# q and k loaded token group first and turned on TensorE, one activation table, issue order from a table: an attention and SoLU feed-forward kernel

## The chip, the cores and the metric

The kernel runs on one core of one Trainium2 chip. The metric is the device time of one execution in microseconds, taken as the median of several runs. The profile is one further execution, recorded by the hardware profiler.

A core has five engines with a queue of instructions each: TensorE (PE; its weight loads are shown apart as PEld), VectorE (DVE), ScalarE (ACT), GpSimd (POOL) and SyncE (SP, which here only issues DMAs). Sixteen DMA engines move data between the chip's memory (HBM) and the on-chip buffer (SBUF). Matmul results land in PSUM, which DVE and ACT read. Each engine works through its queue in order, and an instruction whose semaphore has not come holds up what is queued behind it.

## The reference

Two stages follow each other. The first is attention with 4 batches, 8 heads, 768 tokens and a head size of 64. A query sees the first 8 keys (global) and the 96 keys up to itself (local), with a bias that falls with distance by a slope for each head. The second takes the 3072 x 512 result through a feed-forward layer of width 1024, whose activation is h times softmax(h), followed by a layer norm without offset and a second matrix.

```python
scores = scale * np.matmul(q, k.transpose(0, 1, 3, 2))
...
scores = scores + bias[None, :, :, :]
scores = np.where(keep, scores, -1000000000.0)
...
a = a / (np.sum(a, axis=-1, keepdims=True) + 1e-09)
return np.matmul(a, v).astype(np.float32)
...
h = x @ w_in
h_max = np.max(h, axis=-1, keepdims=True)
e = np.exp(h - h_max)
sm = e / (np.sum(e, axis=-1, keepdims=True) + 1e-09)
solu = h * sm
mu = np.mean(solu, axis=-1, keepdims=True)
var = np.mean((solu - mu) ** 2, axis=-1, keepdims=True)
ln = (solu - mu) / np.sqrt(var + 1e-06) * g_ln
return (ln @ w_out).astype(np.float32)
```

## The kernel before, in words

The work is cut into 12 units: 4 batches of 3 stretches of 256 tokens. Unit `21` is batch 2, stretch 1. All arithmetic on TensorE is in fp16 with fp32 sums. Every piece of work is a step with a name, and steps of unit `21` carry `.21`.

**Loads.** `lq` and `lk` (L296 to L302) each issue two DMAs on SP, one for the even and one for the odd head of each pair. A DMA moves 128 pieces of 2 KB: a piece is 8 tokens (R) of one head, and there are 4 head pairs and 32 token groups. On the source side the pairs are outermost, `j g (r d)`, so partition p holds pair p // 32 and group p % 32. `lv` (L304) issues two DMAs of 1024 pieces of 256 bytes. Each load has two buffers.

**Turning q and k.** `cq` and `ck` (L313) cast to fp16, on POOL but for the first unit, which uses DVE. `tq` and `tk` (L362) then issue a crossbar transpose DMA each on ACT's queue: eight 128 x 128 blocks, one for each token of a group, so that head size comes to the partitions. `kn` (L348) puts the tokens of k back in order, with a copy on POOL. q is left in the turned order, and the score matmuls read it with a stride (L421). Scores therefore hold queries in the order (r, g), the masks are built in that order (`pat`, L201), and the output stores (L601) undo it, eight rows of groups outermost. The first unit is turned on TensorE instead (`pq`, `pk`, L333), with `tq` on ACT and `kn` on DVE copying out of PSUM.

**Attention.** `cv` casts v on POOL into `vd`. `ko` and `vo` (L382, L393, DVE) are copies of k and v in which the first columns are replaced by the global keys and values, that `kg` and `vg` keep for each batch. `sc0` to `sc3` (L408) make the scores of a head pair in PSUM, `ex` (ACT) the exponentials, `mu` (DVE) multiplies with the exponential of bias and mask, `av0` and `av1` (L458) multiply with v, a column of ones giving the sums, `xn` (DVE) divides, `xt` (L495) turns the result on TensorE and `xc` (DVE) copies it to `xT`.

**Feed-forward.** `f10` and `f11` (L514) make h, `e2` (ACT, L526) its exponential, `u` (DVE, L531) the product, `s` (L540) the sums of e, u and u squared on TensorE, `st` and `st2` (DVE) the statistics, `rs` (ACT, L577) one over the root by a Ln and an Exp. `f20` and `f21` (L584) apply the second matrix, whose gain and mean have been folded in beforehand (`gw`, `gm`, `gmc`, `gc`), `o0` and `o1` (ACT) scale and copy out of PSUM, `out0` and `out1` (SP) store.

**Weights.** `l_win` and `l_wout` are loads of 2 MB each on SP; `win0` to `win3` and `gw0` to `gw7` bring them to fp16.

**Buffers in PSUM.** A ring of three two-bank tiles serves scores, `av` and h. Two one-bank tiles (`mm`) serve `xt`, `s`, both `f2`, the first unit's `pq` and `pk`, and `gm`.

**Order.** A planner (L50) runs over all steps when the program is built. Each step has an engine, a duration written by hand, what it depends on, which buffers it takes and gives back, and a priority by unit. The planner gives every engine the step that can start first, by priority within a small window, and the steps are issued in that order.

Of the kernel before, what the change touches and what calls it, by code (L numbers as in the profile page):

```python
# [15 lines left out]
P = 128  # L16


class Step:


    def __init__(self, name, eng, dur, emit, deps=(), take=(), give=(), prio=0.0, dma=0.0):
        self.name, self.eng, self.dur, self.emit = name, eng, dur, emit
        self.deps = [d for d in deps if d is not None]
        self.take, self.give = list(take), list(give)
        self.prio, self.dma = prio, dma
        self.start = self.end = None


class Plan:  # L30
# [6 lines left out]
    LAT = 0.08  # L37
    DMA_LAT = 2.0

# [5 lines left out]
    def add(self, *a, **kw):  # L45
        s = Step(*a, **kw)
        self.steps.append(s)
        return s

    def order(self, window=0.12):  # L50
        free = {p: [0.0] * n for p, n in self.pools.items()}
        givers = {}
        for s in self.steps:
            for g in s.give:
                givers[g] = givers.get(g, 0) + 1
        rel = {}
        clock = {}
        dma_free = {}
        left = list(self.steps)
        done = []  # L60
        while left:
            best = {}
            for s in left:
                if any(d.end is None for d in s.deps):
                    continue
                t = clock.get(s.eng, 0.0)
                for d in s.deps:
                    t = max(t, d.end + (self.LAT if d.eng != s.eng else 0.0))
                ok = True
                need = {}  # L70
                for pool, _ in s.take:
                    need[pool] = need.get(pool, 0) + 1
                for pool, n in need.items():
                    f = sorted(x for x in free[pool] if x is not None)
                    if len(f) < n:
                        ok = False
                        break
                    t = max(t, f[n - 1] + self.LAT)
                if ok:
                    best.setdefault(s.eng, []).append((t, s))  # L80
            assert best, "the plan is stuck: " + ", ".join(s.name for s in left[:12])
            pick = None
            for eng, c in best.items():
                t0 = min(t for t, _ in c)
                t, s = min(((t, s) for t, s in c if t <= t0 + window), key=lambda x: (x[1].prio, x[0]))
                if pick is None or t < pick[0]:
                    pick = (t, s)
            t, s = pick
            for pool, key in s.take:
                f = free[pool]  # L90
                i = min((j for j in range(len(f)) if f[j] is not None), key=lambda j: f[j])
                f[i] = None
                self.slot[(pool, key)] = i
            s.start = t
            clock[s.eng] = t + s.dur
            s.end = t + s.dur
            if s.dma:
                b = max(s.end, dma_free.get(s.eng, 0.0)) + s.dma
                dma_free[s.eng] = b
                s.end = b + self.DMA_LAT  # L100
            for g in s.give:
                givers[g] -= 1
                rel[g] = max(rel.get(g, 0.0), s.end)
                if givers[g] == 0:
                    free[g[0]][self.slot[g]] = rel[g]
            left.remove(s)
            done.append(s)
# [5 lines left out]
def kernel(  # L113
# [21 lines left out]
    R = 8  # L135
# [508 lines left out]
```

## Time and profile before

| | |
|---|---|
| median of 3 runs | 307.53 us (307.14 to 310.0) |
| the profiled execution | 309.56 us |
| its span, first to last instruction | 307.8 us |
| mean granted TensorE clock | 0.818 |
| busy: PE, DVE, ACT, POOL | 170.7, 131.0, 129.6, 64.0 us |
| moved by DMA | 35.42 MB in 60421 packets, 49648 of them under 512 B |
| queue of SP's DMAs (q1) | 29.37 MB, 40.6% of 16 engines |
| queue of ACT's crossbar transposes (q10) | 5.77 MB, 33.3% of 16 engines |

A busy time is the sum over an engine's instructions; the span is longer than any of them. The page cuts the span in 40 slices of 7.7 us and gives the busy share of each in tenths. The clock row is what the throttle granted TensorE, 9 for full speed and 5 for half. In a row of a group stand the line, the engine, the operation, what is written and read, the shape, the count, the busy time, the mean duration in ns, the idle time before it and what ended it. In a row of waits stand who waited for what, the total, the number of waits and the longest. SPq and ACTq are the issue queues of SP and ACT.

### The profile page before, as it was taken

The numbers are of one execution on the slowest core, as the hardware profiler recorded it, in microseconds if no ns is written. First come the engines' busy times: TensorE is split into PE (matmuls) and PEld (weight loads), VectorE is DVE, ScalarE is ACT, GpSimd is POOL, SyncE is SP. The second block draws the span as 40 slices with busy tenths as digits, with TensorE's granted clock in tenths as the row PEclk, the third lists the DMA queues.
The fourth block names the chain that finished last, engine by engine and source line by source line (L and its number), as shares of the span: only waits on it lengthen the run. The fifth ranks groups of instructions, "written<-read, shape, count | busy, mean of one in ns | idle before, by whom it ended". The sixth has DMA issues, their size and how long they took to land.

```text
span 307.8 us, 4520 instructions
## 1 busy us (share of the span) xinstructions
PE 170.7 (55%) x1784; PEld 117.0 (38%) x1784; DVE 131.0 (43%) x323; ACT 129.6 (42%) x165; POOL 64.0 (21%) x91
## 2 busy tenths in 40 slices
PE   0143067374703344691704933069888888989871
PEld 0132046151501233450503522046464657567550
DVE  0072068133405232641207232074786877484530
ACT  5130047171700531442006160046858487876562
POOL 7011140223224213423024110442050400000000
PEclk9999997769585957576655869558997999999998
DMA  2449994999999999996999993198540432102022
GB/s 81 115 135 235 133 316 119 133 121 153 117 122 109 131 144 119 165 141 154 121 121 121 171 139 135 76 149 101 130 102 2 103 36 70 36 34 71 0 70 68
DMA packets 60421, 35.42 MB, mean 115 GB/s; under 512 B 49648, under 2 KB 49648, under 8 KB 60400
## 3 DMA queue, kind: packets, MB, share of 16 engines
q1 hardware_dynamic: 37168, 29.37, 40.6%
q10 hardware_dynamic: 23232, 5.77, 33.3%
q8 instruction: 14, 0.23, 0.4%
q14 instruction: 7, 0.06, 0.1%
HBM read 23.07 MB, written 6.29 MB: 95 GB/s over the span
## 4 chain that ended last, share of the span: by engine, by line
DMA 37%; SPq 23%; PE 18%; DVE 8%; issue 5%; POOL 4%; ACT 4%; ACTq 0%; POOLq 0%; DVEq 0%
DMA ldk<-in_k_dram 20%; DMA ldq<-in_q_dram 13%; SPq L300 11%; SPq L307 8%; PE mm L587 7%; PE ring L519 5%; DMA kt<-c16k 4%; PE mm L551 4%; ACT e L437 3%; SPq L246 2%; DVE u L535 2%; POOL c16q L317 1%; DVE xn L491 1%; DVE ko L388 1%; POOL kn L351 1%
## 5 line engine op out<-in xcount | busy, mean ns | idle before, releaser
L519 PE MATMUL ring<-xT,w_in_sb 128*128 128x256 f16 x384 | 52.8, 299 | 17.5 <-DVE xT L506 15.0
L587 PE MATMUL mm<-gw,u 128*128 128x512 f16 x192 | 51.5, 426 | 13.4 <-DVE st L564 12.4
L528 ACT ACTIVATE e<-ring 128x1024 f16<-128x1024 f32 x24 | 24.5, 1023 | 80.0 <-POOL vd L323 18.6
L519 PEld LDWEIGHTS <-w_in_sb 128*128 128x128 f16 x384 | 40.3, 107 | 27.9 <-ACT w_in_sb L257 14.1
L437 ACT ACTIVATE e<-ring 128x1024 f16<-128x1024 f32 (+1 forms) x48 | 42.7, 958 | 15.7 <-PE ring L422 9.5
L535 DVE TENSOR_TENSOR u<-ring,e 128x1024 f16<-128x1024 f32 x24 | 29.1, 1215 | 41.6 <-ACT e L528 41.6
L587 PEld LDWEIGHTS <-u 128*128 128x128 f16 x192 | 20.1, 107 | 39.6 <-issue 24.3
L422 PE MATMUL ring<-qt,kn 64*128 64x128 f16 x192 | 18.1, 248 | 29.3 <-ACT e L437 23.9
L422 PE MATMUL ring<-qt,ko 64*128 64x128 f16 x160 | 16.2, 244 | 23.5 <-DVE u L535 14.4
L447 DVE TENSOR_TENSOR e<-e,mk 128x1024 f16<-128x1024 f16 x32 | 21.4, 683 | 18.2 <-ACT e L437 18.1
L579 ACT ACT_TABLE_LOAD x12 | 15.4, 1283 | 30.5 <-issue 25.7
L317 POOL CAST c16k<-ldk 128x1024 f16<-128x1024 f32 x11 | 11.4, 1040 | 80.7 <-DMA ldk<-in_k_dram 80.7
L351 POOL COPY kn<-kt 128x1024 f16<-128x1024 f16 x11 | 21.4, 1949 | 22.4 <-PE ring L422 20.0
L469 PE MATMUL ring<-vo,e 128*128 128x65 f16 x160 | 14.8, 210 | 19.2 <-DVE e L447 14.3
L551 PE MATMUL mm<-u 128*128 128x129 f16 x192 | 21.8, 238 | 2.5 <-DVE u L535 2.5
L422 PEld LDWEIGHTS <-kn 64*128 64x128 f16 x192 | 11.0, 107 | 30.9 <-issue 25.0
L323 POOL CAST vd<-ldv 128x512 f16<-128x512 f32 x24 | 14.6, 624 | 34.2 <-DMA ldv<-in_v_dram 32.0
L548 PE MATMUL mm<-ones,e 128*128 128x1 f16 x192 | 21.0, 182 | 0.8 <-ACT e L528 0.8
L551 PEld LDWEIGHTS <-u 128*128 128x128 f16 x192 | 19.7, 116 | 2.9 <-DVE u L535 2.9
L422 PEld LDWEIGHTS <-ko 64*128 64x128 f16 x160 | 9.2, 104 | 29.8 <-issue 25.9
L317 POOL CAST c16q<-ldq 128x1024 f16<-128x1024 f32 x11 | 11.8, 1070 | 41.3 <-DMA ldq<-in_q_dram 32.7
L595 ACT ACTIVATE o<-mm,st 128x512 f32<-128x512 f32 x24 | 15.4, 684 | 9.0 <-issue 7.9
(67 smaller groups left out, 219.3 us busy)
## 6 DMA issues: line engine op xcount, KB each, us to landing
ldq<-in_q_dram SPq DMA_DIRECT2D x24, 256.0 KB
ldk<-in_k_dram SPq DMA_DIRECT2D x24, 256.0 KB
ldv<-in_v_dram SPq DMA_DIRECT2D x24, 256.0 KB
out_dram<-o SPq DMA_DIRECT2D x24, 256.0 KB
w_tmp<-in_moe_w_in_dram SPq DMA_DIRECT2D x1, 2048.0 KB
w_tmp<-in_moe_w_out_dram SPq DMA_DIRECT2D x1, 2048.0 KB
qt<-c16q ACTq DMA_TRANSPOSE x11
kt<-c16k ACTq DMA_TRANSPOSE x11
```

Of the source, the lines that this page charges most:

```text
L300: nc.sync.dma_start(out=t[:, m, :], in_=a)
L307: nc.sync.dma_start(out=t[:, a], in_=v[b][:, tok0 + a * P : tok0 + (a + 1) * P, :].rearrange("h t d -> t h d"))
L317: eng.tensor_copy(out=dst.rearrange("p r m d -> p m r d"), in_=src.rearrange("p m (r d) -> p m r d", r=R))
L351: nc.gpsimd.tensor_copy(out=dst, in_=src)
L422: nc.tensor.matmul(out=t[:, 512 * m + P * c : 512 * m + P * (c + 1)], lhsT=lhs, rhs=rhs, start=(c == (1 if po is None else 0)), stop=(c == ...
L437: nc.scalar.activation(out=e[:, :, lo:], in_=t[:, :, lo:], func=AF.Exp, scale=inv_sqrt_d)
L447: nc.vector.tensor_tensor(out=ev, in0=ev, in1=mb, op=ALU.mult)
L519: nc.tensor.matmul(out=t[:, jj, :], lhsT=w_in_sb[:, c, ts(4 * hf + jj, P)], rhs=x[:, c, :], start=(c == 0 and jj % 2 == 0), stop=(c == NCC ...
L528: nc.scalar.activation(out=e2[plan.slot[("e2", f"{U}{hf}")]].rearrange("p j f -> p (j f)"), in_=t, func=AF.Exp)
L535: nc.vector.tensor_tensor(out=o[:, :, 0:P], in0=t, in1=e, op=ALU.mult)
L551: nc.tensor.matmul(out=t[:, a, 0 : P + 1], lhsT=uv[:, jj, a, 0:P], rhs=uv[:, jj, a, 0 : P + 1], start=False, stop=(a == 1 and hf == 1 and ...
L587: nc.tensor.matmul(out=t, lhsT=uu[plan.slot[("u", f"{U}{i // 4}")]][:, i % 4, a, 0:P], rhs=gw[:, i, :], start=(i == 0), stop=(i == NFC - 1))
```

## The change

- `lq` and `lk` put the token groups outermost on the source side, `g j (r d)`, so partition p holds group p // 4 and pair p % 4.
- All units are turned on TensorE: `pq` and `pk` take a `mm` tile each for eight transposes. `tq` (ACT) and `kn` (ACT, in the first unit DVE) copy out of PSUM into token order, reading with a stride. The crossbar transposes, `kt` and POOL's `kn` are gone, `kn` has two buffers instead of three.
- q is in token order now: the score matmuls read 128 neighbouring columns, the masks use plain token order, and an output store is a plain block of 128 rows.
- A step `tab` at the start asks for the table set that has both exponential and logarithm.
- `cvo` on POOL casts v into `vo` directly; `vo` on DVE only puts the global rows in. The two copies of the global columns, one for each half, become one copy with a repeated source.
- `l_win` is issued by ACT, after mask3.
- `f2` no longer waits for `s`; `s` holds the `u` buffers instead.
- The planner is gone. The steps are issued in the order of a written table, `ORDER`, of 603 names, and a buffer goes to the step that asks next, the one longest free first.

The diff, cut to its core:

```diff
+ORDER = """
+tab ident lq.00 dist lk.00 lv.00 ones mask6 mask3 cq.00 mask4 pq.00 mask0 mask2 lq.01 ck.00 mask5 tq.00 pk.00
+lk.01 mask7 kn.00 l_win lv.01 kg.00 ko.00 sc0.00 mask1 cvo.00 sc1.00 ex0.00 sc2.00 ex1.00 sc3.00 mu0.00 l_g
+ex2.00 mu1.00 lk.02 ex3.00 mu2.00 lq.02 cv.00 l_wout mu3.00 vg.00 vo.00 ck.01 av0.00 av1.00 xn0.00 cq.01 pk.01
+xn1.00 kn.01 pq.01 lk.10 win3 win0 xt.00 ko.01 lq.10 xc.00 tq.01 win2 lv.02 win1 sc0.01 cv.01 sc1.01 sc2.01
+ex1.01 cvo.01 ex2.01 f10.00 mu1.01 ex0.01 mu2.01 lv.12 mu0.01 sc3.01 e20.00 f11.00 vo.01 cq.02 ex3.01 u0.00
+ck.02 pq.02 e21.00 lq.11 mu3.01 pk.02 tq.02 u1.00 av0.01 kn.02 lk.21 av1.01 xn0.01 s.00 xn1.01 gw1 gw7 st.00
+xt.01 gw5 ck.10 xc.01 gw3 st2.00 f11.01 gw4 lk.11 ko.02 cq.10 gw6 gw2 f10.01 lq.12 gw0 rs.00 cvo.02 e21.01 gm
+cv.02 e20.01 u1.01 lv.10 pq.10 gmc cv.12 u0.01 sc0.02 tq.10 sc1.02 pk.10 gc0 ex1.02 s.01 kn.10 mu1.02 sc2.02
+sc3.02 ex0.02 kg.10 ko.10 gc4 ex3.02 sc0.10 ex2.02 sc1.10 mu0.02 f20.00 ex1.10 mu3.02 ex0.10 mu2.02 vo.02 sc2.10
...
+f11.32 st.31 st2.31 rs.31 f10.32 e21.32 u1.32 f21.31 e20.32 u0.32 f20.31 o1.31 out1.31 s.32 o0.31 out0.31 f21.32
+st.32 st2.32 rs.32 f20.32 o1.32 out1.32 o0.32 out0.32
+"""
...
+    def run(self, order):
...
+        free = {p: list(range(n)) for p, n in self.pools.items()}
+        issued = set()
+        for name in names:
+            s = by_name[name]
+            assert all(d.name in issued for d in s.deps + s.after), name
             for pool, key in s.take:
...
+                self.slot[(pool, key)] = free[pool].pop(0)
+            s.emit()
+            issued.add(name)
...
-    pat = [[1, R], [R, G]]
+    pat, npat = [[1, P]], [[-1, P]]
...
     def e_tab():
-        pass
...
+        nc.scalar.preload_act_table_set("natural_log_exp_and_others")
+    plan.add("tab", "ACT", e_tab)
...
+    l_win = plan.add("l_win", "ACT", lambda: e_wload(w_tmp, moe_w_in, NCC), after=[c_mask[3]])
...
-            s4 = src[b].rearrange("(j m) s d -> m j s d", m=2)[m]
-            a = s4[:, tok0 : tok0 + QU, :].rearrange("j (g r) d -> j g (r d)", r=R)
-            nc.sync.dma_start(out=t[:, m, :], in_=a)
...
+            s4 = src[b].rearrange("(j m) s d -> m j s d", m=2)
+            for m in range(2):
+                a = s4[m][:, tok0 : tok0 + QU, :].rearrange("j (g r) d -> g j (r d)", r=R)
+                nc.sync.dma_start(out=t[:, m, :], in_=a)
...
+        def e_castvo(U=U, nb=nb):
+            for a in range(nb):
+                nc.gpsimd.tensor_copy(out=vo[plan.slot[("vo", U)]][:, a, :, 0:D], in_=ldv[plan.slot[("ldv", U)]][:, a])
...
-            nc.scalar.dma_start_transpose(out=dst, in_=src.rearrange("p r m d -> p (r m d)"))
...
+        def e_tev(which, eng, U=U):
             t = mm[plan.slot[("m", which + "p" + U)]].bitcast(FP16)
...
+            src = t.rearrange("p (r g j) -> p j g r", r=R, j=NPAIR)
+            d = (qt if which == "q" else kn)[plan.slot[("qt" if which == "q" else "kn", U)]]
+            dst = d.rearrange("p j (g r) -> p j g r", r=R)
+            if eng == "ACT":
+                nc.scalar.copy(out=dst, in_=src)
...
-                        rhs = qv[lo : lo + D, :, j * 32 + 16 * (c // 2) : j * 32 + 16 * (c // 2) + 16]
+                        rhs = qv[lo : lo + D, j, P * (c // 2) : P * (c // 2 + 1)]
...
-                nc.sync.dma_start(out=out[row : row + P, :].rearrange("(g r) c -> r g c", r=R), in_=osb[plan.slot[("o", f"{U}{a}")]])
...
+                nc.sync.dma_start(out=out[row : row + P, :], in_=osb[plan.slot[("o", f"{U}{a}")]])
```

## The prediction

> **What bounds the kernel now.** I read the page's slices first, then the chain and the waits, then busy time by stage. A first digit of the DMA row near 9 says that the copy engines are busy, not that they are all at work, so the stage windows come last.
>
> ```profile
> PE   0143067374703344691704933069888888989871
> ...
> PEclk9999997769585957576655869558997999999998
> DMA  2449994999999999996999993198540432102022
> ...
> DMA 37%; SPq 23%; PE 18%; DVE 8%; issue 5%; POOL 4%; ACT 4%; ACTq 0%; POOLq 0%; DVEq 0%
> ```
>
> Up to slice 26 (200 us) PE comes and goes and DMA is at 9; after it PE is at 8 to 9 and DMA fades. The chain belongs to DMA and to SP's issue queue. Who waits, over the whole run:
>
> ```profile
> POOL c16k L317 <- DMA ldk<-in_k_dram: 80.7, 11, 17.4
> ...
> POOL c16q L317 <- DMA ldq<-in_q_dram: 32.7, 7, 9.2
> POOL vd L323 <- DMA ldv<-in_v_dram: 32.0, 10, 9.5
> ```
>
> The casts wait for the q and k loads. Why those take 9 to 14 us each shows in the windows (PE, PEld, DVE, ACT, POOL busy, then clock, share of the 16 DMA engines, GB/s):
>
> ```profile
> 3.00:6.00 3.00, 0.00 (x0) 0.00 (x0) 0.00 (x0) 1.62 (x4) 2.73 (x22) 1.00 0.24 89
> ...
> 42.00:45.00 3.00, 2.87 (x26) 2.16 (x24) 2.37 (x3) 1.34 (x2) 2.46 (x2) 1.00 1.06 387
> ...
> 304.00:305.50 1.50, 0.00 (x0) 0.00 (x0) 0.00 (x0) 0.00 (x0) 0.00 (x0) 0.92 0.51 186
> ...
> 42.00:212.00 170.00, 84.87 (x791) 55.91 (x790) 62.26 (x158) 55.89 (x70) 44.96 (x42) 0.69 1.01 136
> 212.00:302.00 90.00, 76.35 (x916) 54.55 (x912) 58.41 (x140) 63.10 (x80) 9.58 (x10) 0.98 0.26 60
> ...
> 215.40:284.90 69.50, 59.33 (x750) 42.58 (x749) 49.91 (x118) 49.45 (x61) 7.42 (x7) 0.98 0.27 65
> ```
>
> 3 to 6 us holds only the first q load, whose source has the 4 head pairs outermost: a quarter of the engines, 89 GB/s. 304 to 305.5 holds only output stores, outermost count 8: half. 42 to 45 is w_out, 128 outermost on both sides, 2 KB packets like q's: all 16, 387 GB/s. So the outermost count sets how many engines a copy gets, and one quarter of them carries every q and k byte. From 212 us PE sets the pace: between the xT copies at 215.4 and 284.9 us lie five units (a unit is 256 tokens of a batch), 13.9 us each, with 11.9 us of PE in each.
>
> **The change, part by part.**
>
> *Loads.* With 32 token groups outermost, q and k get 16 engines by the same reading. One load (two DMAs, 0.52 MB) moves in 1.4 us at 387 GB/s instead of 5.4 to 5.9. By the trace's packet records (2 KB median 84 ns, 256 B median 18 ns) a unit needs (512 x 84 + 2048 x 18 + 256 x 84) ns / 16 = 6.3 us of all engines. SP's issues for a unit: four q and k DMAs of 0.55, two v of 1.85 (the first at 3.73 us), two stores of 0.60: 7.1 us. Both fit under a unit of 13 us; without that cover 7.1 us would be the floor of a unit, far from deciding. Stores stand on SP between the loads of later units; four o buffers let one be two units late before an output copy waits.
>
> *Weights.* l_win leaves SP for ACT, behind mask7. Its issue took 2.09 us on SP; queued behind it are mask1 and the first exps, on which mu and av of unit 00 wait. Scores are ready at about 10.5, so the exps lose some 2 us; if the engines are backed up it is up to the 11.6 us of the longest v issue. Unit 00's attention ends at 17.5 while f1 waits for w_in until 22, so 2 us are hidden and 11.6 would cost 7. l_wout moves up on SP, from 33.98 to behind lq.02, about 18.5 (the first six loads' issues to 13.5, l_g 2.5, two loads 2.4): landed near 28, before ACT reaches gw.
>
> *Crossbar transposes out.* 22 issues leave ACT's queue (median 1.25 and 1.41 us, 35 us or less in all), and 22 transfers leave the engines (queue q10, 33.3% of them). POOL loses kn.
>
> *TensorE transposes in.* 22 groups of 8 (the first unit had its own). Warm price: the chain has the eight L501 transposes in 0.45 us, cold the L337 eight in 1.03. A unit pays 0.9 us, on PE, which is the bound: 10 us in all. Each needs one of two mm banks, shared with xt, s and both f2. A bank is held from the first matmul to the end of the copy: 2 x (0.45 + 1.01) + (0.45 + 0.68) + (1.33 + 0.9) + 2 x (1.73 + 0.69), with some 0.15 of crossing each, is 12 us a unit for two banks, so half used. A pq that waits holds every score behind it on PE's queue, and ACT's exps wait for those. Bounds: 0, or one output copy (0.69 us) ahead of each of 22, 15 us. I take 0 as its own term and let the idle share below carry it.
>
> *Evacuations on ACT, strided.* 22 copies. No row has ACT reading PSUM with a stride. Nearest:
>
> ```profile
> L579 ACT ACT_TABLE_LOAD x12 | 15.4, 1283 | 30.5 <-issue 25.7
> ...
> L506 DVE COPY xT<-mm 128x1024 f16<-128x1024 f16 x12 | 8.2, 682 | 3.3 <-PE mm L501 3.3
> ...
> L346 DVE COPY kn<-mm 128x1024 f16<-128x1024 f16 x1 | 1.2, 1225 | 1.1 <-PE mm L337 1.1
> ...
> L342 ACT COPY qt<-mm 128x1024 f16<-128x1024 f16 x1 | 1.0, 1012 | 3.8 <-PE mm L337 3.8
> ```
>
> On DVE the stride costs 1225 against 682, a factor 1.8; on ACT that would be 1.82 us. But DVE's 1225 is its pace for fp32 too (L535, 1215), the 682 a faster form that ACT does not show: its 1024 elements take 1012 in fp16 and 1029 in fp32. So I take 1.01: 22.2 us, and keep 1.82 (17.8 more, 1.6 a unit) and, downward, nothing.
>
> *One table.* 24 loads of 1.283 go (the first stays): 30.8 us of ACT. ACT's sum is 129.6 - 30.8 + 22.2 = 121.0, 10.1 a unit. The load row stands for its whole price: at 209.31 the load, at 210.61 the Ln, 0.02 us later. The Trainium skill, "ScalarE: Activation LUTs", section "What ACT_TABLE_LOAD costs", adds a drain of about 1.38 us to each; by it 63.9 us would come back, an estimate that the starts in this trace do not bear out.
>
> *POOL and DVE.* POOL: 64.0 - 21.4 (kn, 11 x 1.949) + 20 x 0.624 (cvo) = 55. DVE: 131.0 - 7.6 (L395) - 2.9 - 2.3 (eight copies each of L388 and L397, merged) = 118, 9.9 a unit. Both lie beside PE's 12.8. DVE copies do suffer from POOL: L388 takes 0.16 us at the median and 1.94 at worst, beside a kn of 1.9; a cast is 0.62 to 1.04, so the worst shrinks. The masks' multiplies do not: all 32 lie within 669 to 695 ns. Against moving copies to POOL speaks "SBUF — State Buffer" of the Trainium skill, in its single rule on the shared port pair: a DVE instruction with two SBUF inputs should wait for a POOL instruction that reads. With POOL busy a third of the time and half a cast of waiting, that is an estimate of 0.7 us of DVE a unit; by the row it is 0.
>
> *The sum, in span.*
> 1. To the first f1 matmul. Before: 39.66, after the w_in casts at 37.72. After: the q cast at about 6 (9.74 less 4.0 of transfer), k landed at 7.2 (issued by 3.7, 1.4 of transfer, 2 of landing), scores 3.1 us later as before (15.46 to 18.57), xt 7.3 later (25.9 before): 17.5. w_in goes out behind tq.00 and mask7, about 10.5; with the six loads of units 00 and 01 it makes 4.2 MB at 387 GB/s and 1.05 MB of v at 228 (16 x 256 B / 18 ns), 15.5 us from 2.3: 17.8, plus 2 us as the first load has from last packet to cast, plus 2.1 of casts: 22.
> 2. To the first output copy ACT is in front: ten exps 8.9, four e2 4.1, four evacuations 4.0, eight gw 5.2, rs and gmc 1.0: 23, with small waits 24: 46.
> 3. PE: 12 x (11.9 + 0.9) + gm 1.8 = 155; by then done: units 00 and 01 without f2, parts of 02 and 10, gm: 25. Left 130. PE was busy 59.33 of 69.5 there, 0.85; of its waits in 212 to 302 the largest is L422 on ACT's exps, 5.2 us, beside 19.3 us of table loads on ACT. I let half of the idle time go with them: 0.93, 140 us.
> 4. From the last f2: copy 0.69, store and end some 4.3 (5.8 before, from the copy's end at 302.0 to 307.8; one store on 16 engines instead of two on 8 at 186 GB/s saves some 1.5): 5.
>
> 46 + 140 + 5 = 191, less the chance that PE fills earlier in step 2: I take 190. The profiled run took 309.56 for a span of 307.8; the median of the runs, 307.53, is within 0.3 of the span, so 190 stands for both. With no PE idle at all it is 46 + 130 + 5 = 181, and 6 less if the ramp is PE's too: 175. With the old idle share: 46 + 153 + 5 = 204.
>
> **Rivals.**
> - *ACT and the order become the bound.* Strided copies at 1.82 make ACT 11.7 a unit; with mm banks late (up to 15 us) PE stays at 0.85 or below. 204 to 220. For it: in-order queues that each are 75 to 80% full. Against it: none is above PE.
> - *The loads stay narrow*, if the destination counts otherwise than the stores and loads above suggest. Quarter engines then carry 10.9 (q, k) + 2.3 (v) + 1.3 (out) = 14.5 a unit, x 12, plus 10 of weights and some 28 of start and last unit: 212. Against it: the 42 to 45 row.
> - *PE at half clock, ending slower.* 42 to 212 ran at 0.69, with PE idle again and again. If after the change idle gaps keep the clock at 0.5, step 3 is 260 and the whole 311. It decides from 307.5 - 51 = 256 for 130 of work, a mean of 0.51. Against it: 212 to 302 held 0.98 with PE waits of 1.4 us at most.
>
> **How the numbers follow.** Forecast (PE-bound, 175 to 204): 0.74. ACT and order (204 to 220, a tail above): 0.16. Narrow loads: 0.05. Half clock: 0.03; the last 0.02 lies between. The range runs from 175 to 212: it takes in the idle-share bounds and half of the second case, and leaves out about 0.17. Changes under 1% could not be told from none. Faster by over 1% holds all but half clock and a remnant: 0.96; same 0.01; slower 0.03.
>
> **What would show it.** Loads: windows with q or k alone at a DMA share near 1 and over 300 GB/s, casts that no longer wait. Transposes: 176 more on PE at 0.45 for eight. Evacuation: tq and kn at 1.01, not 1.8. Table: one ACT_TABLE_LOAD. Start: first f1 near 22, first output copy near 46. Step 3: PE busy above 0.9 and clock near 1 from 46 on. I am wrong if PE idles over 15% there, if the clock falls below 0.9, or if casts still wait for ldk.

## The result, and the profile after

On one chip the kernel before took 308.76 us (median of 4) and the changed one 180.64 us (median of 4, 179.17 to 182.84): a ratio of 0.583, 95% interval 0.576 to 0.590. One of the four (182.84 us) ran in a slower state of the chip, as did one or two executions of some variants below: the ratios leave such executions out, the medians hold them, and without them no variant's median would move by more than 0.8 us. The forecast was 190.0 with a range of 175 to 212. The profiled execution took 179.17 us with a span of 177.4; all times of day below are in that span.

The slices of the changed kernel, and the shares of its chain:

```profile
PE   0443769799794989999999999999999999999990
...
PEclk9999988999999999999999999999999999999999
DMA  5999999999379779998199400530101111003023
...
PE 63%; ACT 10%; DVE 10%; DMA 9%; issue 3%; SPq 2%; ACTq 0%
```

A slice is now 4.4 us. PE stands at 9 from slice 15 (67 us) to the last but one, where the kernel before stayed at 8 to 9 only after 200 us. The chain, which belonged to DMA and to SP's issue queue, is PE's. DMA is at 9 in slices 1 to 9, comes and goes after that, and is at 5 or less from slice 22 on.

The waits of the whole run (engine, line and what ended the wait: us in total, times, longest):

```profile
ACT e L511 <- PE ring L502: 20.1, 17, 4.1
POOL cq L308 <- PE mm L332: 15.2, 3, 5.2
...
POOL ck L308 <- DMA ldk<-in_k_dram: 6.5, 2, 5.0
```

The k casts, which waited 80.7 us for their loads, now wait 6.5 (the casts of v, whose loads the change left as they were, still wait 19.1). The longest wait is ACT's for PE: the engine that sets the pace is the one waited for. The second says the same of POOL, which may write the next q tile only when PE has turned an earlier one.

The windows (start and end, length, then PE, PEld, DVE, ACT and POOL busy, PE clock, share of the DMA engines, GB/s):

```profile
3.00:6.00 3.00, 0.60 (x6) 0.61 (x7) 0.72 (x1) 0.49 (x2) 2.67 (x20) 1.00 0.99 317
22.00:46.00 24.00, 19.99 (x278) 15.90 (x278) 18.29 (x35) 21.25 (x29) 8.78 (x12) 0.93 0.97 288
46.00:172.00 126.00, 121.63 (x1589) 90.90 (x1589) 96.59 (x240) 85.77 (x119) 38.20 (x47) 1.00 0.42 127
```

From 3 to 6 us the engines carry loads at a share of 0.99 instead of 0.24, and 317 GB/s instead of 89. From 46 to 172 us PE is busy for 121.63 of 126 us, 0.965, at full clock; no other engine is above 0.77.

The rows that price the added and removed work (busy, mean ns | idle before, and what ended it):

```profile
L429 DVE TENSOR_TENSOR e<-e,mk 128x1024 f16<-128x1024 f16 x32 | 24.4, 789 | 4.1 <-ACT e L419 4.1
...
L340 ACT COPY qt<-mm 128x1024 f16<-128x1024 f16 x12 | 12.1, 1012 | 0.7 <-PE mm L332 0.7
...
L332 PE MATMUL mm<-ident,ck 128*128 128x128 f16 x96 | 8.2, 234 | 1.6 <-DVE ck L308 1.3 <-DVE xT L488 0.3
...
L231 ACT ACT_TABLE_LOAD x1 | 1.3, 1283 | 0.7 <-PEq L606 0.7
```

The strided evacuations cost 1.01 us, not 1.82 (kn's eleven: 1016 ns). There is one table load. The 192 transposes of q and k, 96 of each, take 16.4 us of busy time, overlapped matmuls counted in full.

The start, in the chain (start, length, what):

```profile
9.75 10.81 DMA w_tmp<-in_moe_w_in_dram
...
24.53 3.31 PE ring L502 x16
```

w_in goes out at 9.75 and has landed at 20.56; between the two lines shown the chain has ACT evacuate a q tile (from 21.54), cast a part of w_in and take an exponential, and the first f1 matmul comes at 24.53. The last f2 ends at 173.26 and the span at 177.4.

### The profile page after: what moved, and what is told of

The parts are those of the page before. It is cut to its first block, busy times and chain, and to the rows that moved or that the text cites. A ratio compares the mean times of both kernels' runs of the same rounds, so it can differ in the third digit from the quotient of the medians.

```text
span 177.4 us, 4800 instructions
## 1 busy us (share of the span) xinstructions
PE 151.7 (86%) x1960; PEld 113.9 (64%) x1960; DVE 126.6 (71%) x295; ACT 119.2 (67%) x163; POOL 59.6 (34%) x100
## 4 chain that ended last, share of the span: by engine, by line
PE 63%; ACT 10%; DVE 10%; DMA 9%; issue 3%; SPq 2%; ACTq 0%
PE ring L502 24%; PE mm L570 19%; PE mm L534 6%; DMA w_tmp<-in_moe_w_in_dram 6%; ACT e L419 4%; PE ring L404 3%; PE mm L332 3%; DMA ldq<-in_q_dram 3%; PE ring L453 2%; DVE u L518 2%; PE ring L451 2%; DVE e L429 2%; ACT e L511 2%; PE mm L483 2%; SPq L293 1%
## 5 line engine op out<-in xcount | busy, mean ns | idle before, releaser
L502 PE MATMUL ring<-xT,w_in_sb 128*128 128x256 f16 x384 | 46.6, 278 | 4.6 <-DVE xT L488 2.9
L502 PEld LDWEIGHTS <-w_in_sb 128*128 128x128 f16 x384 | 37.6, 99 | 11.1 <-issue 4.7
L570 PE MATMUL mm<-gw,u 128*128 128x512 f16 x192 | 44.7, 379 | 0.0
L570 PEld LDWEIGHTS <-u 128*128 128x128 f16 x192 | 17.9, 98 | 18.5
L429 DVE TENSOR_TENSOR e<-e,mk 128x1024 f16<-128x1024 f16 x32 | 24.4, 789 | 4.1 <-ACT e L419 4.1
L578 ACT ACTIVATE o<-mm,st 128x512 f32<-128x512 f32 x24 | 16.5, 688 | 10.5 <-PE mm L570 10.3
L321 POOL CAST vo<-ldv 128x512 f16<-128x512 f32 x20 | 14.1, 719 | 20.1 <-PE ring L453 15.0
L308 POOL CAST cq<-ldq 128x1024 f16<-128x1024 f32 x11 | 12.3, 1119 | 17.0 <-PE mm L332 15.2
L473 DVE TENSOR_TENSOR xn<-ring,rl 128x512 f16<-128x512 f32 x24 | 16.6, 691 | 0.8
L453 PE MATMUL ring<-vd,e 128*128 128x65 f16 x192 | 14.4, 197 | 2.7 <-DVE e L431 2.4
L534 PEld LDWEIGHTS <-u 128*128 128x128 f16 x192 | 15.9, 96 | 0.8 <-issue 0.4
L531 PEld LDWEIGHTS <-e 128*128 128x128 f16 x192 | 15.9, 96 | 0.6
L308 POOL CAST ck<-ldk 128x1024 f16<-128x1024 f32 x11 | 11.9, 1090 | 11.9 <-DMA ldk<-in_k_dram 6.5
L453 PEld LDWEIGHTS <-e 128*128 128x128 f16 x192 | 12.2, 99 | 5.0 <-DVE e L431 3.4
L340 ACT COPY kn<-mm 128x1024 f16<-128x1024 f16 x11 | 11.2, 1016 | 5.4 <-PE mm L332 5.4
## 6 DMA issues: line engine op xcount, KB each, us to landing
w_tmp<-in_moe_w_in_dram ACTq DMA_DIRECT2D x1, 2048.0 KB, 10.8
```

The costliest lines, as they stand in the source:

```text
L308: eng.tensor_copy(out=dst.rearrange("p r m d -> p m r d"), in_=src.rearrange("p m (r d) -> p m r d", r=R))
L429: nc.vector.tensor_tensor(out=ev, in0=ev, in1=mb, op=ALU.mult)
L453: nc.tensor.matmul(out=o, lhsT=e[:, m, QU * a + P : QU * a + QU], rhs=vd[plan.slot[("vd", U)]][:, a, h, :], start=(first_in_bank and not t ...
L502: nc.tensor.matmul(out=t[:, jj, :], lhsT=w_in_sb[:, c, ts(4 * hf + jj, P)], rhs=x[:, c, :], start=(c == 0 and jj % 2 == 0), stop=(c == NCC ...
L531: nc.tensor.matmul(out=t[:, a, P + 1 : P + 2], lhsT=e[:, jj, ts(a, P)], rhs=ones1, start=first, stop=False, skip_group_check=True)
L534: nc.tensor.matmul(out=t[:, a, 0 : P + 1], lhsT=uv[:, jj, a, 0:P], rhs=uv[:, jj, a, 0 : P + 1], start=False, stop=(a == 1 and hf == 1 and ...
```

## The experiments

Theory A is that of the prediction: narrow loads bound the kernel before, the crossbar transposes came second, and once both are gone PE is the bound and the order and the table set decide how near to it the kernel comes. Theory B holds the crossbar transposes to be the main cost, the loads' width to be little. Theory C holds that the written order and the table set bring the gain. Where an expectation names a theory otherwise, it says what it is. "Pace" is the time from the first output copies to the last one, divided by the units between. The first four variants were timed once each, beside one execution of the kernel before at 306.54 us. A variant of the changed kernel keeps the order that was written for the whole change, or nearly so (a_planner apart): part of its loss can be an order that no longer fits, and no run separates that.

**b_wide: the kernel before with wide loads alone.**

```diff
-            a = s4[:, tok0 : tok0 + QU, :].rearrange("j (g r) d -> j g (r d)", r=R)
+            a = s4[:, tok0 : tok0 + QU, :].rearrange("j (g r) d -> g j (r d)", r=R)
...
-                src = t.rearrange("p (r j g) -> p j g r", r=R, j=NPAIR)
+                src = t.rearrange("p (r g j) -> p j g r", r=R, j=NPAIR)
...
-            src = kt[plan.slot[("kt", U)]].rearrange("p r (j g) -> p j g r", j=NPAIR)
+            src = kt[plan.slot[("kt", U)]].rearrange("p r (g j) -> p j g r", j=NPAIR)
...
-                        rhs = qv[lo : lo + D, :, j * 32 + 16 * (c // 2) : j * 32 + 16 * (c // 2) + 16]
+                        rhs = qv[lo : lo + D].rearrange("p r (g j) -> p j r g", j=NPAIR)[:, j, :, 16 * (c // 2) : 16 * (c // 2) + 16]
```

> The kernel before with only the load pattern changed (token groups outermost); crossbar transposes, planner and table loads stay. Theory A (a quarter of the DMA engines carried q and k, and that was the bound): the loads need 6.3 us of all engines a unit and the 22 transposes at most 1024 packets x 72 ns x 2 / 16 = 9 us more, so PE's 13.9 us a unit takes over: 195 to 220 us, and the POOL casts' waits on ldq and ldk fall from 113 us to under 30. Theory B (the crossbar transposes held the engines): little changes, 270 us or more, with kn and c16 still waiting.

Measured: 228.34 us, 78 less than before. That is 8 above the top of A's range and far below B's. One window and its largest wait:

```profile
42.00:100.00 58.00, 42.92 (x459) 28.92 (x457) 44.09 (x93) 29.56 (x36) 33.05 (x28) 0.87 1.10 242
```

```profile
POOL c16k L317 <- DMA ldk<-in_k_dram: 23.8, 9, 6.6
```

The wait for k falls from 80.7 to 23.8 us, not to nothing: with the crossbar's transfers still there, the engines are full until 100 us (share 1.10), and PE is busy for 42.92 of those 58 us.

The last pair of lines of the edit costs something by itself. With the groups outermost and q left in turned order, the score matmuls read every fourth column of q, where the kernel before reads runs of 16 neighbours and the changed kernel 128. Their rows here and in the changed kernel:

```profile
L422 PE MATMUL ring<-qt,kn 64*128 64x128 f16 x192 | 23.1, 285 | 7.8 <-ACT e L437 6.5
...
L404 PE MATMUL ring<-qt,kn 64*128 64x128 f16 x192 | 14.1, 226 | 2.9 <-ACT e L419 1.6
```

With overlaps counted once, PE is busy with scores for 25.6 us here, 17.3 in b_turn and 15.4 in the changed kernel. So the 78 us are the gain of wide loads less this loss. b_wide_turn and a_xq carry the same loss (24.5 and 23.8 us of scores).

**b_turn: the kernel before with all units turned on PE, narrow loads kept.**

```diff
-        if first:
+        if True:
             tpq = plan.add(f"pq.{U}", "PE", 0.9, (lambda f=e_pturn: f("q")), deps=[cq, c_ident], take=[("m", "qp" + U)],
```

> The kernel before with only the turning changed (all units by TensorE, q copied out by ACT, k by DVE); loads stay on a quarter of the engines, planner and table loads stay. Theory A: the quarter still carries 10.9 + 2.3 + 2.7 = 16 us a unit, 190 us and about 40 of start and end: 225 to 250 us, casts still wait for ldk. Theory B: with the transposes gone the loads run free: 190 to 215 us.

Measured: 268.52 us, 38 less than before, 18 above the top of A's range and 53 above B's. The casts still wait:

```profile
POOL c16k L317 <- DMA ldk<-in_k_dram: 41.9, 8, 7.4
```

For q it is 33.1 us more. Theory B falls. The two parts in the old kernel are worth 78 and 38.

**b_wide_turn: both edits, old planner, old table loads.** The diff is that of the two runs above.

> The kernel before with both: wide loads and TensorE turning; planner and table loads stay. Theory A: PE's 13.9 + 0.9 us a unit and a start of about 25: 205 to 215 us, some 30 above the changed kernel, which is what order, table set and POOL copies brought. Theory C (the written order carries most of the gain): 240 us or more.

Measured: 211.68 us, in A's range. Three quarters of the whole gain (94.9 of 126.3, to 180.23) are there without the written order or the table set, so C falls as the main cause. What is left is 31 us, for the order, the table set and everything else in which this run differs from the changed kernel: its scores cost PE 9 us more (see b_wide), DVE and not ACT copies k out of PSUM, w_in is issued by SP, and the copies of v and of the global columns, the wait of f2 for s and the stores are the old ones. Against b_wide, which reads q in the same way, turning both on PE brings 16.7 us.

**a_narrow: the changed kernel with narrow loads.**

```diff
-                a = s4[m][:, tok0 : tok0 + QU, :].rearrange("j (g r) d -> g j (r d)", r=R)
+                a = s4[m][:, tok0 : tok0 + QU, :].rearrange("j (g r) d -> j g (r d)", r=R)
...
-            src = t.rearrange("p (r g j) -> p j g r", r=R, j=NPAIR)
+            src = t.rearrange("p (r j g) -> p j g r", r=R, j=NPAIR)
```

> The changed kernel with the old load pattern (head pairs outermost) and the turning adapted; all else as changed. Theory A: a quarter of the engines carries 10.9 + 2.3 + 1.3 = 14.5 us a unit: 205 to 235 us, PE idle a quarter of the time and casts waiting for ldq and ldk. Theory C: the order hides it, 180 to 195 us.

Measured: 264.9 us, 85 more than the changed kernel. C's value is out, and A's own is 30 too low. Its largest wait (that for k is 50.3 us), one window, and the chain:

```profile
POOL cq L308 <- DMA ldq<-in_q_dram: 53.0, 6, 14.1
```

```profile
100.00:160.00 60.00, 38.01 (x469) 29.00 (x470) 24.32 (x60) 26.40 (x33) 20.91 (x27) 0.78 0.45 137
```

```profile
SPq 42%; DMA 24%; PE 23%; ACT 3%; POOL 3%; issue 2%; DVE 1%; POOLq 0%
```

From 3 to 6 us the first load moves at 91 GB/s, a share of 0.26, as before the change, and later PE is busy for 38.01 us of 60. I had counted what a quarter of the engines can carry and nothing more. The chain's largest share is SP's issue queue: an in-order queue on which a v load took a median of 2.44 us to issue (0.59 in the changed kernel) and at most 12.5. The issues of SP add up to 179 us here, 74 in the changed kernel and 185 in the kernel before; b_turn and b_wide_turn, which differ in the loads and the order of q, have 192 and 86. So narrow loads cost twice, in the engines and on the queue of the engine that issues. The second part is read from these rows; no run tried it by itself.

The other runs were timed in several rounds, each beside the kernel before; differences are to a_again, and where the chip was another the ratios bear them out.

**a_again: the changed kernel once more, as base.**

> The changed kernel once more, as the common base of the runs beside it: 178 to 183 us by either theory.

Measured: 180.23 us, ratio 0.582 [0.577, 0.587].

**a_tables: the table set not asked for.**

```diff
     def e_tab():
-        nc.scalar.preload_act_table_set("natural_log_exp_and_others")
+        pass
```

> The changed kernel without the step that asks for the common table set, so that the 24 table loads of 1.28 us come back on ACT. Theory A (PE sets the pace and ACT has slack, 67% busy): ACT rises to 150 of some 180 us, and part of it shows, because each pair of loads lies between s and the output copy that frees an mm bank: 186 to 200 us, PE busy in the middle down to 0.85 to 0.92. Rival (the loads lie in ACT's idle time and the gain of 0.85 to 0.96 in PE's share came from the order alone): 180 to 184 us.

Measured: 199.35 us, ratio 0.646 [0.640, 0.652], 19.1 above the base, within A's range. Twenty-four loads are back, and ACT is busy 149.5 us against 119.1 (L563 has the other dozen):

```profile
L562 ACT ACT_TABLE_LOAD x12 | 15.4, 1283 | 0.2
```

```profile
46.00:172.00 126.00, 111.79 (x1463) 82.73 (x1461) 89.30 (x216) 100.88 (x123) 39.73 (x47) 0.95 0.41 118
```

```profile
PE mm L483 <- ACT o L578: 3.9, 4, 1.6
PE mm L531 <- ACT o L578: 2.8, 1, 2.8
```

ACT's busy time from 46 to 172 us rises from 85.77 to 100.88, and PE's share falls to 0.89. The last fence, the largest of PE's waits between 46 and 170 us, shows how (L570 and L332 wait 4.1 us more for the same): the load stands ahead of the row factors, the output copy is late, and it holds a mm bank that the next xt, s, f2 or transposes need. ACT was no bound by its sum and cost PE time all the same.

**a_double: every q and k transpose done twice.**

```diff
-            for r in range(R):
+            for r in list(range(R)) * 2:
```

> The changed kernel with each group of eight transposes of q and k done twice into the same tile (192 more matmuls that change nothing). Theory A (PE is the bound from 46 us on): 22 groups x 0.45 us = 10 us more, 188 to 193 us. Rival (ACT or DVE sets the pace and PE only looks busy): 180 to 184 us.

Measured: 185.43 us, ratio 0.598 [0.592, 0.604], 5.2 above the base, between the two expectations. The row of k's (q's reads 14.0):

```profile
L332 PE MATMUL mm<-ident,ck 128*128 128x128 f16 x192 | 14.4, 235 | 0.9 <-DVE ck L308 0.6 <-DVE xT L488 0.3
```

The rows grow by 12.0 us, but overlapped matmuls are counted in full there; PE's own busy time grows by 7.5, and of these 5.2 reach the end, some two thirds. That fits PE as the bound most of the time, with slack for the rest.

**a_vodve: v copied into vo on DVE again, POOL's second cast left out.**

```diff
         def e_castvo(U=U, nb=nb):
-            for a in range(nb):
-                nc.gpsimd.tensor_copy(out=vo[plan.slot[("vo", U)]][:, a, :, 0:D], in_=ldv[plan.slot[("ldv", U)]][:, a])
+            pass
...
+            nc.vector.tensor_copy(out=t[:, 0:nb, :, 0:D], in_=vd[plan.slot[("vd", U)]][:, 0:nb, :, 0:D])
```

> The changed kernel with the copies of v into vo taken back from POOL to DVE, as before the change: POOL loses 20 casts of 0.62 us or more, DVE gains some 7.6 us of copies. If POOL's reads hold up DVE's mask products (789 ns in the mean after the change, 683 before) but PE is the bound, those return toward 690 ns and the time stays within 2 us of the changed kernel, 178 to 184 us. If the contention lay on the path, 2 to 5 us faster; if DVE is the bound, 3 to 8 us slower.

Measured: 180.84 us, ratio 0.584 [0.580, 0.589]: the base's time. POOL falls to 46.1 us, DVE comes to 128.8. The masks' products take 762 ns on average and 1.52 us at most. The changed kernel shows 789 in one execution and 743 in another (a_again), so no fall can be told: the casts that stay on POOL are enough for the delay, and it does not reach the end. Where the v copy runs is worth nothing here.

**a_planner: the changed kernel's steps in the order of a planner of the old kind.** The durations and priorities of the steps are my own, after those of the kernel before, so the loss is the price of this planner and need not be that of the old one.

```diff
+    UNIT = {"lq": (0.12, -2.8), "lk": (0.12, -2.8), "lv": (0.12, -2.7), "cq": (1.4, -1.8), "ck": (1.4, -1.8), "cv": (1.4, -1.7),
...
+        while left:
+            best = {}
+            for s in left:
...
+                t, s = min(((t, s) for t, s in c if t <= t0 + window), key=lambda x: (x[1].prio, x[0]))
+                if pick is None or t < pick[0]:
+                    pick = (t, s)
...
-            s.emit()
+        for s in done:
+            s.emit()
```

> The changed kernel with its steps in the order that the old planner gives (durations and priorities as in the kernel before, the new steps with measured ones), instead of the written table. Theory A: both loads, table set and TensorE turning stay, so what is lost is PE's share in the middle, 0.96 back to 0.85 to 0.90, and some of the start: 190 to 200 us. Rival (the order brought nothing, the table set and the loads all): 179 to 184 us.

Measured: 207.41 us, ratio 0.668 [0.663, 0.674], 27 above the base and 7 above the range. The work is the same; its window and its largest wait:

```profile
46.00:172.00 126.00, 111.55 (x1412) 83.53 (x1412) 86.04 (x214) 80.00 (x108) 32.62 (x41) 0.96 0.41 119
```

```profile
ACT st L629 <- DVE st L623: 27.9, 11, 4.4
```

PE's share falls to 0.885. ACT stands 27.9 us in its queue at the row statistics, waiting for DVE, where the written order has 7.9 (L562). What PE itself waits for there is spread out: its largest wait from 46 to 172 us is 3.1, for exponentials. The first output copy starts at 49.8 us (48.4 in the changed kernel), so little was lost in the ramp: the pace is 13.6 us a unit instead of 11.1.

The four runs by order and table set:

| | planner | written order |
|---|---|---|
| loads of two table sets | 211.7 (b_wide_turn) | 199.4 (a_tables) |
| one set | 207.4 (a_planner) | 180.2 (a_again) |

By these times the set alone brings 4 and the order alone 12, together 31. All three are taken from b_wide_turn, which was timed once and differs in the further points named there. If its 9 us of PE for strided scores reached the end in the proportion of a_double, some two thirds, each of the three would be some 6 us smaller: that is an estimate. Either way the two together are worth more than the sum of the parts; how much each is worth alone is not shown.

**a_win: w_in's load first of all.**

```diff
-tab ident lq.00 dist lk.00 lv.00 ones mask6 mask3 cq.00 mask4 pq.00 mask0 mask2 lq.01 ck.00 mask5 tq.00 pk.00
-lk.01 mask7 kn.00 l_win lv.01 kg.00 ko.00 sc0.00 mask1 cvo.00 sc1.00 ex0.00 sc2.00 ex1.00 sc3.00 mu0.00 l_g
+tab ident lq.00 dist lk.00 l_win lv.00 ones mask6 mask3 cq.00 mask4 pq.00 mask0 mask2 lq.01 ck.00 mask5 tq.00 pk.00
+lk.01 mask7 kn.00 lv.01 kg.00 ko.00 sc0.00 mask1 cvo.00 sc1.00 ex0.00 sc2.00 ex1.00 sc3.00 mu0.00 l_g
...
-    l_win = plan.add("l_win", "ACT", lambda: e_wload(w_tmp, moe_w_in, NCC), after=[c_mask[3]])
+    l_win = plan.add("l_win", "ACT", lambda: e_wload(w_tmp, moe_w_in, NCC))
```

> The changed kernel with the w_in load issued at once by ACT, ahead of the masks, instead of at 9.75 us. The first f1 matmul stands at 24.5 us, after the last w_in cast. If w_in's landing sets it, f1 comes at 22 to 23 us and the whole is 1 to 3 us faster, 177 to 180 us. If the first unit's attention sets it, or q and k are held up by w_in on the same engines, no gain or 1 to 3 us slower, 180 to 184 us.

Measured: 186.12 us, ratio 0.600 [0.596, 0.604], 5.9 above the base.

```profile
10.05 0.69 DVE L308 CAST cq<-ldq 128x1024 f16<-128x1024 f32 x1 [10.05 <-DMA ldq<-in_q_dram]
```

The first q cast starts at 10.05 us instead of 4.62: 2.1 MB of weights share all 16 engines with it. The first f1 comes at 30.1 instead of 24.5, and those 5.6 us pass about one to one to the end. So the place of l_win behind the masks is part of what the change is worth, though it looks like a detail.

**a_xq: q by the crossbar on ACT's queue again, from the second unit on.**

```diff
-        "ldq": 2, "ldk": 2, "ldv": 2, "cq": 2, "ck": 2, "qt": 2, "kn": 2, "ko": 3, "vd": 3, "vo": 3,
+        "ldq": 2, "ldk": 2, "ldv": 2, "cq": 2, "ck": 2, "qt": 5, "kn": 2, "ko": 3, "vd": 3, "vo": 3,
...
+        def e_xq(U=U):
+            nc.scalar.dma_start_transpose(out=qt[plan.slot[("qt", U)]], in_=c16["q"][plan.slot[("cq", U)]].rearrange("p r m d -> p (r m d)"))
...
+        else:
+            tq = plan.add(f"tq.{U}", "ACT", e_xq, deps=[cq], take=[("qt", U)], give=[("cq", U)])
```

> The changed kernel with q turned by a crossbar transpose DMA on ACT's queue from the second unit on (in the old token order, with the old masks, stores and five qt buffers), k still by TensorE. PE loses 11 groups of eight, some 5 us, ACT 11 copies of 1.01 us for 11 issues of 1.25. Theory A (the loads were the fault, not the crossbar, and PE is the bound): 175 to 180 us. Rival (the transposes, 0.2 us a packet at the worst before, hold up the loads and ACT's queue): 183 to 200 us, with waits on qt and on loads.

Measured: 204.68 us, ratio 0.662 [0.658, 0.665], 24 above the base and 5 above the highest expectation. The largest of PE's waits, and the window:

```profile
PE ring L412 <- DMA qt<-cq: 15.8, 2, 15.1
```

```profile
46.00:172.00 126.00, 115.62 (x1415) 85.17 (x1412) 92.63 (x227) 80.45 (x111) 36.39 (x47) 0.97 0.65 141
```

One transposed q tile, among the loads of the ramp, makes the scores wait 15.1 us, and PE is busy only 9.4 of the 24 us from 22 to 46 (19.99 in the changed kernel). The first f1 matmul comes at 37.47, 13 us later than there, about half of the loss. From 46 to 172 us the share is 0.918. PE is spared eleven groups of eight transposes, some 5 us at 0.45, but its score matmuls read every fourth column of q again:

```profile
L412 PE MATMUL ring<-qt,kn 64*128 64x128 f16 x192 | 22.0, 285 | 1.7 <-DVE kn L344 1.3
```

They cost PE 23.8 us instead of 15.4, more than it is spared. So the 24 us are not the crossbar's alone. qt also has five buffers; these parts were not tried apart. (The 0.2 us a packet of the expectation is not in the trace of the kernel before: its transposes' packets took 72 ns on average and 3.7 us at the longest.)

**a_early: w_in still earlier, without passing the first loads.**

```diff
-tab ident lq.00 dist lk.00 lv.00 ones mask6 mask3 cq.00 mask4 pq.00 mask0 mask2 lq.01 ck.00 mask5 tq.00 pk.00
+tab ident lq.00 dist lk.00 lv.00 ones mask6 l_win mask3 cq.00 mask4 pq.00 mask0 mask2 lq.01 ck.00 mask5 tq.00 pk.00
...
-xn1.00 kn.01 pq.01 lk.10 win3 win0 xt.00 ko.01 lq.10 xc.00 tq.01 win2 lv.02 win1 sc0.01 cv.01 sc1.01 sc2.01
+xn1.00 win0 win1 kn.01 pq.01 lk.10 win3 win2 xt.00 ko.01 lq.10 xc.00 tq.01 lv.02 sc0.01 cv.01 sc1.01 sc2.01
```

> The changed kernel with the w_in load issued behind the first mask (about 6 us: q has landed, k nearly) instead of at 9.75, and its four casts put ahead of kn.01 on ACT and next to each other on DVE. If a delay of the first f1 matmul passes to the end one to one, as the run with w_in at 0.76 us showed in the other direction (f1 at 30.1 instead of 24.5, end 5.9 later), f1 at 22.5 to 23.5 makes 178 to 179.5 us, a gain at the edge of what can be told. If the v and next q, k loads that w_in now overtakes hold up unit 01, 180 to 183 us.

Measured: 180.74 us, ratio 0.584 [0.581, 0.587]: no gain. In its profile (an execution of 182.85 us) the first casts of w_in start at 18.04 instead of 20.59, and the first f1 matmul where it was:

```profile
24.53 1.87 PE L502 MATMUL ring<-xT,w_in_sb 128*128 128x256 f16 x8 [0.68 <-ACT e L419]
```

It waits for a ring tile that an exponential of the next unit holds, with the weights cast by 20.73 and the first unit's xT copied by 22.86. The weights were not the only thing that came ready at 24.5. None of the eleven variants beat the changed kernel.

## Why the prediction was right, and where its sizes were off

The mechanism held in the main: the loads got all engines, PE became the bound, and its share decided the time. Three things in it were wrong and hid behind the right total: a wait that step 1 left out, a reading of the masks' products, and a reading of the DMA row. The sum of 191 was 13.6 us above the span of 177.4: 12.7 of it in step 3, 0.9 in the last.

| step | predicted | measured |
|---|---|---|
| q cast, k landed | 6, 7.2 | 4.62, 6.96 |
| w_in issued, cast | 10.5, 19.8 | 9.75, 20.59 |
| first f1 matmul | 22 | 24.53 |
| first output copy | 46 | 48.4 |
| PE's work, and what is left of it from 46 us | 155, 130 | 151.7, 122.9 |
| PE's share in that stage | 0.93 | 0.965 |
| from the last f2 to the end | 5 | 4.1 |

*Step 3, the mis-sized term.* Some three fifths of the miss are work: PE's whole sum was 3.3 us less than forecast, and 28.8 us of it were done by 46 us where I had counted 25. At my share of 0.93 the 122.9 us would take 132.2, not 140. The rest is the share: 122.9 / 0.965 is 127.3. I took the old share of 0.85 and let half of its idle time go with the table loads. a_tables and a_planner show that both the set and the order mattered: with either of them taken away the share is 0.89. The order's worth had no term of its own in my sum. With 46 + 127.3 + 4.1 the span comes out: 177.4.

*Step 1, a wait that was left out.* The loads are as forecast (0.99 of the engines, 317 GB/s), and w_in landed within 1 us of the estimate. f1 was 2.5 us late, and what came last was neither of the two things that I had counted: xT was copied by 23.44 and w_in cast by 24.04, and then f1 still waited for a ring tile, until an exponential of unit 01, which the written order puts ahead of it, ended at about 24.5. a_early shows the same wait alone. My step had no term for the ring.

The first unit's attention was also later than the 17.5 I had: its xt lies at 20.4 to 21.4. Two delays show. The first is in the masks' products. Lines of DVE and POOL from 12.4 us on:

```profile
12.40 0.29 DVE L431 TENSOR_TENSOR e<-e,mk 128x256 f16<-128x256 f16 x1 [1.33 <-ACT e L419]
...
12.47 1.12 POOL L308 CAST ck<-ldk 128x1024 f16<-128x1024 f32 x1 [1.44 <-DMA ldk<-in_k_dram]
...
12.61 1.26 DVE L432 TENSOR_TENSOR e<-e,mk 128x512 f16<-128x512 f16 x1
```

The product of 512 columns takes 1.26 us beside the cast, where later, without one, it takes 0.41; the next one of 256 columns, at 13.79 beside another cast, takes 1.12 instead of the 0.29 of the first line. With a third, these lose some 2.1 us. The second is the order: xt's input was ready at 19.46, but PE was still turning q of unit 01, which stands ahead of xt, and both mm banks were held until a copy of k ended at 20.39. No run tried either delay by itself. The first output copy was 2.4 late as well. The sum does not show what that cost, since PE had more done by then than I had counted; a_win, where f1 came 5.6 us later and the end 5.9, suggests that it passed on.

*Masks' products and POOL.* Here I misread the kernel before. That all 32 products of 1024 columns lay within 669 to 695 ns said nothing of a cast beside them: none of the 32 overlapped an instruction of POOL at all. Of the sixteen of 256 columns, which I did not look at, one did overlap a copy, and took 2.04 us where the smallest took 0.27. In the kernel before:

```profile
203.86 2.10 POOL L351 COPY kn<-kt 128x1024 f16<-128x1024 f16 x1 [2.33 <-PE ring L422]
...
204.07 2.04 DVE L449 TENSOR_TENSOR e<-e,mk 128x256 f16<-128x256 f16 x1
```

In the changed kernel the mean of the 32 is 789 ns (743 in a_again) and the largest 1.49 us; of the ten that overlap a cast, three are as short as the rest. The Trainium skill, "SBUF — State Buffer", section "Who interferes with whom", states that a DVE instruction with two SBUF inputs contends with a GpSimd instruction that reads SBUF; the lines above agree with it. It cost less than the estimate from that page (0.7 us a unit): L429 grew by 3.0 us and L432 by 2.1, 0.4 a unit. And from the ramp on it lies beside PE: a_vodve, with 13.5 us less on POOL, is no faster.

*The DMA row.* The prediction took a 9 there to mean engines that are busy but not all at work. The row is a mean over the 16 engines, so a 9 says that nearly all were busy, and a load on a quarter of them cannot give it. From 42 to 212 us the share was 1.01 in the kernel before, but 0.40 in b_turn and 0.43 in a_narrow, which have the narrow loads without the crossbar transposes:

```profile
42.00:212.00 170.00, 114.22 (x1357) 82.63 (x1354) 95.63 (x233) 94.33 (x118) 33.26 (x40) 0.86 0.40 118
...
42.00:212.00 170.00, 108.88 (x1266) 82.50 (x1266) 75.23 (x188) 79.01 (x104) 40.45 (x53) 0.81 0.43 123
```

So the row of 9s was the narrow loads and the transposes together. What showed the narrow loads were the windows with one load alone (0.24 of the engines), and that reading held.

*DVE's sum* was forecast at 118 and is 126.6. The products give 4.6 of the 8.6 (L431 fell by 0.5). The merged copies give 3.4: I had 5.2 coming back, and while ko's fell from 6.5 to 2.9 us, vo's rose from 5.1 to 6.9, for one copy of 8x1024 takes 681 ns where the mean of 8x512 was 286. DVE is at 0.77 in the main stage; no run tried the copies by themselves.

*ACT* was forecast at 121.0 and is 119.2: evacuations at 1.01, one table load. a_tables gives the price of a load: 24 of them raise ACT's busy time by 30.4 us (24 x 1.283 is 30.8), and the next instruction follows at once. Two lines of ACT's timeline there:

```profile
81.87 1.28 ACT L562 ACT_TABLE_LOAD   x1
83.16 0.20 ACT L562 ACTIVATE st<-st 128x2 f32<-128x2 f32 x1
```

The load ends at 83.15 and the logarithm starts at 83.16. The exponential before the load had ended at 81.85. The further drain of about 1.38 us that "ScalarE: Activation LUTs" of the Trainium skill, section "What ACT_TABLE_LOAD costs", states doesn't show there, on either side of the load. To the whole the loads were worth 19.1 us, not 30.8, for ACT had slack.

*The mm banks and crossbar.* The bound of 0 to 15 us for waiting banks was rightly left at 0 for the main stage of the changed kernel: from 46 to 172 us the largest of PE's waits comes to 2.0 us, and no wait for a bank to more than 0.3. In the ramp xt stood about 1 us behind unit 01's transposes and their banks (above). In a_tables they appear, 10.8 us for output copies. That turning on PE is cheaper than the crossbar shows in b_wide against b_wide_turn (16.7 us for q and k); a_xq (24 for q) points the same way but has the strided scores in it. What the transposes cost on PE shows in a_double (5.2 for as many again).

*Rivals.* Strided copies at half pace: refuted by the L340 rows. Loads still narrow: by the 3 to 6 us window; a_narrow shows what it would have been, 264.9, and that my price of 212 for it, which counted only engine time, was 53 too low. PE at half clock: the clock was 1.00 in the main stage.

## What to carry to other kernels

Look for a window in which one load runs alone: its DMA share and GB/s show how many of the engines it has, and its outermost dimension is the first thing to look at when they are low. The DMA row of the whole run needn't show it. Here the fix of one index order gave 78 us in the old kernel and its loss cost 85 in the new one. A narrow copy also goes with longer issues behind it, so price its queue as well as its engines. When you change the order in which data lie, follow it to whoever reads them: here it put a stride into the matmuls until q was also brought back into token order. Once one engine is the bound, order and small work on engines off the path can be worth more together than apart; a_tables shows one way, an output copy that is late and gives back its bank late.

## What the runs showed of the hardware

- The issue time of a load depends on what else the queue carries. The same v load, with 256 B rows, took 0.59 us at the median in the changed kernel and 2.44 with narrow q and k loads on SP's queue, 2.84 in the kernel before. My 1.85 in the prediction was a symptom of the narrow loads, not a price of v. Source lines of a_narrow and of the changed kernel (ns, smallest/median/largest):

```profile
L300 SPq DMA_DIRECT2D ldv<-in_v_dram x24: 368/2444/12547, 3.4 to 195.2; - x24
```

```profile
L300 SPq DMA_DIRECT2D ldv<-in_v_dram x24: 367/587/5099, 3.4 to 109.5; - x24
```

- A matmul whose moving operand is read at every fourth column takes PE longer. In a_xq sixteen score matmuls in a row take 0.98 to 1.07 us, in the changed kernel 0.55; the rows read 285 and 226 ns.
- A transfer through the crossbar among other loads can be late: one made the scores of a_xq wait 15.1 us.
- The PEclk row reads 9 in the first slices (1.00 in the window from 3 to 6 us), and yet all five groups of eight transposes up to 20.44 us took 1.01 to 1.06 us each, where most later ones take 0.61 (0.45 to 0.55 in the chain, which ends a group where the next work starts). The record of the clock in this trace begins only at 21.43 us, so the row doesn't say how the matmuls before that run.
